# Gated mix of grouped attention and an MLP: two key tiles per stretch of values, eight PSUM banks in rotation, keys split in the second stage

## The chip, the core and the metric

The kernel runs on one core of one Trainium2 chip. A core has a matrix engine (TensorE, PE in the profile, whose weight loads are listed apart as PEld), a vector engine (VectorE, DVE), an activation engine (ScalarE, ACT), GpSimd (POOL) and SyncE (SP), which here only issues transfers. Each engine works through its own list of instructions in order, and waits for the others through semaphores. Matrix products land in PSUM, which has eight banks of 128 x 512 fp32 numbers; PE writes there, DVE and ACT read from there, and everything else is in SBUF or in the chip's memory. The metric is the time of one execution in device microseconds (us).

## What is computed

The input `x` has 2048 tokens of 448 features. Three things are made of it: a gate, attention with 16 query heads that share one key and one value head of 28 features, and an MLP mixer. The output is the gated mix of the last two.

```python
g = sigmoid((x * gate_w).sum(-1, keepdims=True))
# attention: q has 16 heads of 28, k and v have one
scores = einsum("bhqd,bkd->bhqk", q, k) * 28 ** -0.5
a = (softmax(scores) @ v, heads side by side) @ wo
# mixer: a layer norm, 448x448 with gelu, a shift of four channel groups
# by +1, -1, +2, -2 tokens, 448x448, and then
x1 = x + hs
b = x1 + gelu(layernorm(x1) @ w3) @ w4      # 448 -> 1792 -> 448
out = g * a + (1 - g) * b
```

## The kernel before, in words

**Numbers.** Most products are made in fp32r, a one-pass form of fp32 with fewer bits. To keep the accuracy an operand is split into a high part (rounded to fp32r) and a low part (the rest), and three products are added: high x high, high x low, low x high. Names end in `h` and `l` accordingly (`kH`, `kL`, `qh`, `ql`, `w3h`, `w3l`, `onh`, `onl`). The values are multiplied in plain fp32, whose matmul the trace shows as two instructions.

**Order.** The schedule is manual: each engine's instructions run in the order in which the program writes them, and the tile pools add the waits. A tile with `bufs=1` has one buffer, so its next use waits for the last reader of the one before.

**First stage** (to about 130 us). Queries, keys, values and the gate come out of one product per block of 512 tokens; they are written to a scratch tensor `qd` in the chip's memory by `q_out`. Then comes the first half of the mixer (`stage_w1`, `stage_w2`). At its end the keys are fetched: `load_k(b)` (L328) brings block `b` of the keys from `qd` into the tile `kf` with eight DMAs on SP, four copies of the keys at partitions 0, 32, 64 and 96, and `split_k(b)` (L334) makes `kH` and `kL` of it on POOL (L336, L337). The four blocks go through the one `kf`. `kf` is set to 1.0 once, which leaves two rows of ones beside the 28 key features. After them on POOL come the memsets that `split_w_high` (L106) needs for the weights `w3`, and after them on SP the next weight blocks (`load_w34`, L550).

**Second stage, the MLP** (about 130 to 420 us). Four token blocks `b`, 14 feature tiles `f` each: `w3_part` makes a tile of gelu outputs (L130 to L134, L631 to L633), `w4_part` (L641 to L643) adds the tile of two steps before into four accumulators. Between them lie the layer norm of the next block (at f = 9 to 11, through the one-buffer tile `xn`), and work that prepares attention: at b = 1 the tile `khd`, the first `MK` keys set out four times as a block diagonal, and the first queries (`q_load`, `q_split`); from b = 2 on, through `fill`, the maxima of the first unit.

**Attention** (about 420 to 981 us). A unit `u` is a block of 512 tokens and a group of four heads; there are 16. The four heads lie at the partitions 0, 32, 64, 96. For each of the 16 key tiles (128 keys) a step makes:

- scores: for each head one bank, three products of 28 to 30 rows each, on four row tiles of the array at once (L828);
- exponentials: one ACT instruction for each bank, into an SBUF tile `p` (L832);
- values: `pv_group` multiplies the `p` of the key tile two steps before (`LAG`) with `vext`, in which the values stand behind a column of ones; the four heads lie on four column tiles of the array (L808). One bank, `pv`, collects all 16 key tiles of a unit, and DVE then copies it to `o` (L736). Its rows 0, 32, 64, 96 are the sums of the exponentials.

Seven banks rotate among scores and the single products; `pv` has the eighth. The two spare rows of `kH` and `qh` take the row maximum off the scores: `max_part` (L200) takes the maximum over the first `MK` = 64 keys, one product for each of four token tiles (L204, L205), at four different steps of the unit before, and `max_end` writes it to the query tile by DMA. Should a sum be over `LIMIT`, a branch at the end repeats attention with exact maxima.

The sums go to memory and come back as reciprocals on all partitions (`sums_begin`, `recip`: L738, L745, L747, L749); `norm` (L752) multiplies `o` by them on DVE (L754) and splits the result on POOL (L757, L758). At four later steps, `wo_job` (L763) multiplies a token tile with `wo`, again in three products (L769 to L771), and DVE weighs it with the gate and adds it (L778). In the first unit, four last products of the MLP (`w4_job`) stand there. The last unit is normalized by transposes on PE (`tail_sums`, `tail_on`, `tail_back`, `tail_low`).

What decides when a step can start, in a few lines:

```python
bs = [bank(f"s_{4 * k + j}") for j in range(4)]     # next four of the rotation
for i in range(3):
    for j in range(4):
        ... nc.tensor.matmul(bs[j], w, a, start=(i == 0), stop=(i == 2), ...)
if kt in WO_AT: ... wo_job(u - 1, t)
if u + 1 < NU and kt in m_at: ... max_part(u + 1, t, bank)
if k >= LAG:
    pv_group(k - LAG)
```

## Time and profile before

| | us |
|---|---|
| median of 3 runs (lowest, highest) | 994.31 (994.22, 994.57) |
| the profiled execution | 995.8 |
| its span in the profile | 994.0 |
| PE busy | 970.8 |
| ACT busy | 651.9 |
| DVE busy | 287.1 |
| POOL busy | 107.5 |

The profile is taken from one execution. The first page gives the busy time of each engine, the chain of work that ended last (followed backwards from the last instruction), and groups of instructions by line and form. A group's row reads: line, engine, operation, output <- inputs, sizes, count | busy us, mean ns of one | idle time of the engine ahead of it, and what ended it. A row of the timeline reads: start, length, engine, line, operation, with the idle time ahead of it and what ended that in brackets; instructions of one form that overlap are merged (x4). Matmuls are pipelined, so their lengths overlap: the distance from one start to the next is what a matmul takes. A row of busy times by stretch reads: from:to, length, then for PE, PEld, DVE, ACT and POOL the busy us and the instructions, the granted clock of PE, the busy share of the DMA engines, GB/s. A row of waits reads: who <- for whom: us in total, times, longest.

### The profile page before, as it was taken

The numbers are of one execution on the slowest core, as the hardware profiler recorded it, in microseconds if no ns is written. First come the engines' busy times: TensorE is split into PE (matmuls) and PEld (weight loads), VectorE is DVE, ScalarE is ACT, GpSimd is POOL, SyncE is SP. The second block draws the span as 40 slices with busy tenths as digits, with TensorE's granted clock in tenths as the row PEclk, the third lists the DMA queues.
The fourth block names the chain that finished last, engine by engine and source line by source line (L and its number), as shares of the span: only waits on it lengthen the run. The fifth ranks groups of instructions, "written<-read, shape, count | busy, mean of one in ns | idle before, by whom it ended". The sixth has DMA issues, their size and how long they took to land.

```text
span 994.0 us, 18445 instructions
## 1 busy us (share of the span) xinstructions
PE 970.8 (98%) x7251; PEld 562.5 (57%) x7251; DVE 287.1 (29%) x572; ACT 651.9 (66%) x1266; POOL 107.5 (11%) x134
## 2 busy tenths in 40 slices
PE   9999949999999999999999999999999999999997
PEld 6788838888888888843333333333333333333333
DVE  4663424631431431212222222212222221222112
ACT  5542315432232232299999999999998999999895
POOL 2241320100000520040000000000000000000000
PEclk9999969999999999999999999999999999999999
DMA  9703334130210300010000010000010000110001
GB/s 322 244 27 79 114 98 121 44 87 1 40 41 2 77 3 11 1 49 24 13 24 14 19 54 13 24 13 20 27 41 23 14 24 12 42 33 3 12 13 41
DMA packets 38750, 46.19 MB, mean 46 GB/s; under 512 B 8880, under 2 KB 27008, under 8 KB 38656
## 3 DMA queue, kind: packets, MB, share of 16 engines
q1 hardware_dynamic: 35632, 39.47, 13.4%
q10 hardware_dynamic: 3024, 5.47, 1.6%
q8 instruction: 59, 0.97, 0.4%
q14 instruction: 35, 0.29, 0.1%
HBM read 32.85 MB, written 11.67 MB: 45 GB/s over the span
## 4 chain that ended last, share of the span: by engine, by line
PE 94%; DMA 2%; SPq 1%; POOL 1%; DVE 0%; issue 0%; ACT 0%; POOLq 0%; DVEq 0%; ACTq 0%
PE pv L808 25%; PE bank L828 23%; PE acc L642 4%; PE acc L641 4%; PE acc L643 4%; PE g L131 4%; PE g L132 4%; PE g L130 4%; PE bank L769 2%; PE bank L204 2%; SPq L332 1%; PE g L133 1%; PE bank L771 1%; PE g L134 1%; PE bank L770 1%; PE h L130 1%
## 5 line engine op out<-in xcount | busy, mean ns | idle before, releaser
L832 ACT ACTIVATE p<-bank 128x512 f32<-128x512 f32 x1024 | 515.3, 640 | 47.9 <-PE bank L828 45.6
L808 PE MATMUL pv<-p,vext 128*32 128x512 f32 x2048 | 272.9, 604 | 0.0
L828 PEld LDWEIGHTS bank<-qh,kH 30*128 30x128 f32 x1024 | 51.7, 181 | 214.4 <-ACT p L832 212.9
L631 ACT ACTIVATE gh<-g 128x512 fp32r<-128x512 f32 x55 | 32.8, 597 | 183.6 <-PE g L134 183.6
L828 PE MATMUL bank<-qh,kH 30*128 30x512 f32 x1024 | 133.1, 494 | 0.4 <-ACT p L832 0.4
L828 PE MATMUL bank<-qh,kL 28*128 28x512 f32 x1024 | 105.7, 391 | 0.0
L828 PE MATMUL bank<-ql,kH 28*128 28x512 f32 x1024 | 105.6, 388 | 0.0
L633 DVE TENSOR_TENSOR gl<-gf,gh 128x512 fp32r<-128x512 f32 x55 | 38.5, 700 | 165.3 <-ACT gf L632 165.3
L808 PEld LDWEIGHTS pv<-p,vext 128*32 128x32 f32 x2048 | 40.6, 108 | 76.5 <-issue 62.8
L642 PE MATMUL acc<-w4l,gh 128*128 128x448 f32 x220 | 80.4, 366 | 0.0
L641 PE MATMUL acc<-w4h,gh 128*128 128x448 f32 x220 | 80.3, 365 | 0.0
L643 PE MATMUL acc<-w4h,gl 128*128 128x448 f32 x220 | 80.2, 365 | 0.0
L778 DVE SCALAR_TENSOR_TENSOR ot<-bank,gg,ot 128x448 f32<-128x448 f32 x44 | 30.1, 684 | 161.2 <-PE bank L771 122.6
L131 PE MATMUL g<-al,w3h 128*128 128x512 f32 x168 | 66.4, 395 | 0.0
L205 DVE TENSOR_REDUCE mr<-bank 128x4 f32<-128x256 f32 x60 | 25.6, 426 | 141.2 <-PE bank L204 141.2
L130 PE MATMUL g<-ah,w3h 128*128 128x512 f32 x168 | 66.3, 395 | 0.0
L132 PE MATMUL g<-ah,w3l 128*128 128x512 f32 x168 | 66.3, 395 | 0.0
L757 POOL CAST onh<-on 128x512 fp32r<-128x512 f32 x15 | 9.2, 611 | 493.0 <-DVE on L754 458.7
L828 PEld LDWEIGHTS bank<-ql,kH 28*128 28x128 f32 x1024 | 52.6, 185 | 9.1
L828 PEld LDWEIGHTS bank<-qh,kL 28*128 28x128 f32 x1024 | 51.9, 185 | 0.0
L641 PEld LDWEIGHTS acc<-w4h,gh 128*128 128x128 f32 x220 | 41.3, 188 | 4.7
L642 PEld LDWEIGHTS acc<-w4l,gh 128*128 128x128 f32 x220 | 41.3, 188 | 4.1
(196 smaller groups left out, 1096.2 us busy)
## 6 DMA issues: line engine op xcount, KB each, us to landing
qd<-qf ACTq DMA_DIRECT2D x16, 256.0 KB
qr<-qd SPq DMA_DIRECT2D x16, 256.0 KB
rb<-rd SPq DMA_DIRECT2D x15, 256.0 KB
x<-in_x_dram SPq DMA_DIRECT2D x4, 896.0 KB
xd<-xt SPq DMA_DIRECT2D x16, 224.0 KB
w34raw<-in_w_dram SPq DMA_DIRECT2D x7, 512.0 KB
out_dram<-ot SPq DMA_DIRECT2D x15, 224.0 KB
w34raw<-in_w_dram SPq DMA_DIRECT2D x7, 448.0 KB
```

What stands on the lines that cost most here:

```text
L130: nc.tensor.matmul(ps, wh[:, c, :], ah[:, c, :], start=(c == 0), stop=False)
L131: nc.tensor.matmul(ps, wh[:, c, :], al[:, c, :], start=False, stop=False)
L132: nc.tensor.matmul(ps, wl[:, c, :], ah[:, c, :], start=False, stop=False)
L631: nc.scalar.activation(gh, ps, AF.Gelu_apprx_tanh)
L633: nc.vector.tensor_sub(gl, gf, f32(gh))
L641: nc.tensor.matmul(ps, gh[:, tok], w4h[i][:, k, :], start=(f == 0), stop=False)
L642: nc.tensor.matmul(ps, gh[:, tok], w4l[i][:, k, :], start=False, stop=False)
L643: nc.tensor.matmul(ps, gl[:, tok], w4h[i][:, k, :], start=False, stop=(f == stop))
L778: nc.vector.scalar_tensor_tensor(ot_of[n], ps, gg[:, n:n + 1], before, op0=ALU.mult, op1=ALU.add)
L808: nc.tensor.matmul(pv[32 * j:32 * j + 32, :], vext[:, kt, :], ps[j], start=(kt == 0), stop=(kt == NT - 1), tile_position=(0, 32 * j))
L828: nc.tensor.matmul(bs[j], w, a, start=(i == 0), stop=(i == 2), tile_position=(32 * j, 0))
L832: nc.scalar.activation(p, bs[j], AF.Exp, scale=SCALE)
```

## The change

- **Keys split later.** `load_k` and `split_k` leave the end of the first stage. They run in the second token block of the MLP, at f = 0 to 7, each block of keys through a tile of the tag `xn`, which is set to 1.0 each time. `khd` and the first queries move from b = 1 to b = 2, the first unit's maximum from b = 2 on to b = 3.
- **Maxima in one stop.** `MK` goes from 64 to 32, and `max_all` puts the four token tiles into one bank, followed by one DVE reduction; it runs once in a unit, at v = 2.
- **Attention in stretches.** A stretch `v` has two key tiles; a unit has eight. It issues the scores and exponentials of both, then at v = 2 the maximum, at v = 4 to 7 a product with `wo`, and then `values`, the values of the stretch before: both key tiles into one bank. DVE copies the first stretch's sum to `o` in SBUF and adds the others to it. All eight banks rotate; a bank goes to the end of the list when its reader is issued. (`DRAIN` is empty, so `late_exps` issues nothing.)
- **Products with `wo` in fp32.** `norm` no longer splits; `wo_job` multiplies the fp32 `on` with the fp32 `wof`, 32 tokens on each of four column tiles. The splits of `wo` and `on` and `tail_low` are gone. In the tail, DVE adds the last sum to `o` in place of four ACT copies.

```diff
-MK = 64
+MK = 32
-    def max_part(u, t, tile_of): ...
+    def max_all(u, ps):
+        mx_of[u] = late.tile([P, 4, 4], F32, tag="mr", bufs=1, name=f"mr_{u}")
+        for t in range(4):
+            nc.tensor.matmul(ps[:, t * P:(t + 1) * P], qh_of[u][:, t * P:(t + 1) * P], khd, start=True, stop=True)
+        nc.vector.reduce_max(mx_of[u].rearrange("p j t -> p t j"), ps.rearrange("p (t j k) -> p t j k", t=4, j=4), axis=AX.X)
...
-        def load_k(b):
+        def load_k(b, kf):
+            kf_of[b] = kf
+            nc.gpsimd.memset(kf, 1.0)
...
-            split_k(t) if t < 2 else None
-            load_k(t + 1) if t < 2 else None
         stage_w2(NB - 2, third)
-        split_k(2)
-        load_k(3)
-        split_k(3)
...
+                if b == 1 and f in (0, 2, 4, 6):
+                    load_k(f // 2, s2a.tile([P, 512], F32, tag="xn", bufs=1, name=f"kf_{f // 2}"))
+                if b == 1 and f in (1, 3, 5, 7):
+                    split_k(f // 2)
-                if b == 1 and f == 1:
+                if b == 2 and f == 1:
                     nc.gpsimd.memset(f32(khd), 0.0)
...
-        banks = [mm_tile("bank_0"), mm_tile("bank_1"), misc_tile("bank_2")]
+        banks = [mm_tile("bank_0"), mm_tile("bank_1"), misc_tile("bank_2"), max_tile("bank_7")]
...
         def norm(u, o, rb):
-            (on, onh, onl: product on DVE, split on POOL)
+            on_of[u] = s3.tile([P, 512], F32, tag="on", bufs=2, name=f"on_{u}")
+            nc.vector.tensor_mul(on_of[u], o, rb)
...
         def wo_job(u, t, end=None):
-            nc.tensor.matmul(ps, onh[:, tok], woh[:, g, :], start=True, stop=False)
-            nc.tensor.matmul(ps, onh[:, tok], wol[:, g, :], start=False, stop=False)
-            nc.tensor.matmul(ps, onl[:, tok], woh[:, g, :], start=False, stop=True)
+            ps = take()
+            for j in range(4):
+                tok = slice(t * P + 32 * j, t * P + 32 * j + 32)
+                nc.tensor.matmul(ps[32 * j:32 * j + 32, 0:D], on_of[u][:, tok], wof[:, g, :],
+                                 start=True, stop=True, tile_position=(0, 32 * j))
...
+        def values(u, v, add=True):
+            pv = take()
+            for kt in (2 * v, 2 * v + 1):
+                ps = p_of.pop((u, kt))
+                for j in range(4):
+                    nc.tensor.matmul(pv[32 * j:32 * j + 32, :], vext[:, kt, :], ps[j],
+                                     start=(kt % 2 == 0), stop=(kt % 2 == 1), tile_position=(0, 32 * j))
+            if v == 0:
+                o_of[u] = s3.tile([P, 512], F32, tag="o", bufs=2, name=f"o_{u}")
+                nc.vector.tensor_copy(o_of[u], pv)
+            elif add:
+                nc.vector.tensor_add(o_of[u], o_of[u], pv)
+            else:
+                return pv
+            banks.append(pv)
...
+        for k in range(NU * NV):
+            u, v = divmod(k, NV)
+            if v == 6 and u + 2 < NU:
+                q_begin(u + 2)
+                q_fetch(u + 3)
+            for kt in (2 * v, 2 * v + 1):
+                exps(u, kt, scores(u, kt))
+            if v == 2 and sums:
+                norms.append(recip(*sums.pop()))
+            if v == 3 and norms:
+                norm(*norms.pop())
+            if v == M_AT and u + 1 < NU:
+                ps = take()
+                max_all(u + 1, ps)
+                banks.append(ps)
+                max_end(u + 1)
+            job = None
+            if v in WO_AT:
+                if u:
+                    job = wo_job(u - 1, WO_AT.index(v))
+                else:
+                    w4_job(WO_AT.index(v))
+            if job:
+                wo_add(*job)
+            if k:
+                values(*divmod(k - 1, NV))
+                if v == 0:
+                    sums.append(sums_begin(u - 1, o_of[u - 1]))
...
         for t in range(4):
-            nc.scalar.copy(o[:, toks[t]], pv[:, toks[t]])
+            nc.vector.tensor_add(o[:, toks[t]], o[:, toks[t]], pv[:, toks[t]])
```

More of the change, by code (lines that the diff above doesn't have):

```diff
@@ L314, in gated_mix_kernel @@
         nc.gpsimd.memset(vT, 0.0)
-        kf = s1b.tile([P, 512], F32, name="kf")
-        nc.gpsimd.memset(kf, 1.0)
         def rest(g, n, b):
@@ L775, in wo_job, with wo_add @@
             if end:
[L776 removed]
+                end(t, n, ps[:, 0:D], before)
+                banks.append(ps)
                 return
[L778 removed]
+            return n, g, ps, before
+        def wo_add(n, g, ps, before):
+            nc.vector.scalar_tensor_tensor(ot_of[n], ps[:, 0:D], gg[:, n:n + 1], before, op0=ALU.mult, op1=ALU.add)
+            banks.append(ps)
             if g == NG - 1:
                 nc.sync.dma_start(out[0, n * P:(n + 1) * P, :], ot_of[n])
[L782 to L785 removed]
         weigh_x1(NT - 4, NT)
@@ L797, in w4_job @@
             nc.vector.scalar_tensor_tensor(x1[:, n, :], ps, gi[:, n:n + 1], x1[:, n, :], op0=ALU.mult, op1=ALU.add)
-        p_of, pv_of, sums, norms = {}, {}, [], []
-        def pv_group(k):
-            u, kt = divmod(k, NT)
-            if kt == 0:
-                pv_of[u] = max_tile(f"pv_{u}")
-            pv = pv_of[u]
-            ps = p_of.pop(k)
-            for j in range(4):
-                nc.tensor.matmul(pv[32 * j:32 * j + 32, :], vext[:, kt, :], ps[j],
-                                 start=(kt == 0), stop=(kt == NT - 1), tile_position=(0, 32 * j))
-            if kt == NT - 1 and u < NU - 1:
-                sums.append(sums_begin(u, pv_of.pop(u)))
@@ new lines, in gated_mix_kernel, with scores, exps @@
+        p_of, o_of, sums, norms = {}, {}, [], []
+        NV = 8
+        def scores(u, kt):
+            bs = [take() for j in range(4)]
+            for i in range(3):
+                for j in range(4):
+                    for _, _, w, a in score(u, bs[j], j, slice(kt * P, (kt + 1) * P), i=i):
+                        nc.tensor.matmul(bs[j], w, a, start=(i == 0), stop=(i == 2), tile_position=(32 * j, 0))
+            return bs
+        def exps(u, kt, bs):
+            ps = p_of[u, kt] = {}
+            for j in READ:
+                ps[j] = s3.tile([P, 512], F32, tag="p", bufs=PB, name=f"p_{u}_{kt}_{j}")
+                if j in DRAIN:
+                    nc.vector.tensor_copy(ps[j], bs[j])
+                else:
+                    nc.scalar.activation(ps[j], bs[j], AF.Exp, scale=SCALE)
+                banks.append(bs[j])
```

117 lines of the change are left out of this document (32 added, 85 removed).

## Prediction

> **What bounds the kernel now.** I read the page first: the shares of the engines and the chain that ended last.
>
> ```profile
> span 994.0 us, 18445 instructions
> PE 970.8 (98%) x7251; PEld 562.5 (57%) x7251; DVE 287.1 (29%) x572; ACT 651.9 (66%) x1266; POOL 107.5 (11%) x134
> PE 94%; DMA 2%; SPq 1%; POOL 1%; DVE 0%; issue 0%; ACT 0%; POOLq 0%; DVEq 0%; ACTq 0%
> L832 ACT ACTIVATE p<-bank 128x512 f32<-128x512 f32 x1024 | 515.3, 640 | 47.9 <-PE bank L828 45.6
> ```
>
> PE holds the end nearly everywhere, so a saving counts only where PE stops waiting or issues less. The last row, the 1024 exponentials, says that ACT is almost as full inside attention; averages do not settle which binds there. The busy time by stretches does (columns: PE, weight loads, DVE, ACT, POOL, then the granted clock): the end of the first stage, a stretch of the MLP, one unit of attention, and twelve us near the end.
>
> ```profile
> 132.00:144.00 12.00, 0.00 (x0) 0.00 (x0) 0.00 (x0) 0.00 (x0) 3.85 (x5) 0.54 0.24 73
> 144.00:150.00 6.00, 5.75 (x14) 4.50 (x15) 3.56 (x7) 3.46 (x6) 1.45 (x6) 0.50 0.67 224
> 212.00:282.00 70.00, 70.00 (x328) 61.25 (x327) 24.06 (x45) 17.28 (x32) 1.21 (x2) 1.00 0.12 29
> 529.00:564.00 35.00, 35.00 (x340) 13.36 (x341) 7.79 (x18) 32.27 (x65) 1.89 (x2) 1.00 0.06 18
> 949.00:961.00 12.00, 11.76 (x121) 4.42 (x116) 1.03 (x3) 12.00 (x26) 0.74 (x2) 1.00 0.08 25
> ```
>
> There are two places to win: 12 us without any PE work, followed by 6 us at half clock; and attention, where PE is full and ACT has some 3 us of 35 free.
>
> **The key split leaves the first stage.** Waits between 105 and 150 us, then the timeline there:
>
> ```profile
> POOL kH L336 <- DMA kf<-qd: 23.4, 3, 8.0
> PE g L133 <- POOL w3h L106: 13.6, 1, 13.6
> ```
>
> ```profile
> 130.24 0.39 PE L132 MATMUL g<-ah,w3l 128*128 128x512 f32 x1
> ...
> 140.16 0.61 SPq L550 DMA_DIRECT2D w34raw<-in_w_dram  x1
> ...
> 142.57 1.26 POOL L337 TENSOR_TENSOR kL<-kf,kH 128x512 fp32r<-128x512 f32 x1
> 143.89 1.57 POOL L106 MEMSET w3h<- 64x256 f32 x6
> ...
> 144.25 0.79 PE L133 MATMUL g<-ah,w3h 128*128 128x512 f32 x1 [13.62 <-POOL w3h L106]
> 144.70 0.83 ACT L105 CAST w3h<-w34raw 128x768 fp32r<-128x768 f32 x1 [24.11 <-DMA w34raw<-in_w_dram]
> ```
>
> PE stands from 130.24 to 144.25 for a memset (six take 1.57 us) that lies on POOL behind the fourth key split; POOL waited three times, 23.4 us, for key rows, which pass through one buffer in eight small DMAs a block. With the key work gone from there the memset runs as soon as POOL reaches it. The gain is 144.25 - 130.24 - 0.23 (the usual step to the next matmul, shown below) = 13.8 us. The clock fell in the hole: 14 matmuls took 5.75 us; at 0.23 they take 3.2, so 2.5 us more come back. Sum -16.3.
>
> What is late next is the second weight block. Its transfer was issued at 140.16, behind the key DMAs on SP, and its cast began at 144.70, 4.5 us later. Without them SP issues it when its buffer comes free, near 121, and the cast starts near 126; PE needs it only after the 22 products of two tiles (22 x 0.23 = 5.1 us from 128.4). Cost 0, at worst a few us of rest wait (rival 3).
>
> In its new place, the second token block of the MLP, the split issues per key block a memset, eight SP DMAs and two POOL operations. The old chain needed about 10 us a block, so 41 us in all. The row 212 to 282 shows POOL busy for 1.2 of 70 us there, and SP has nothing to issue until that block's f = 11, some 55 us in. The borrowed tile `xn` is wanted by DVE's layernorm at f = 10, 50 us in: 9 us of cover, cost 0; without it, the overrun would delay the next block's activations. `khd`, `qr_0` and the first maximum move a block later, still a block ahead of attention: 0.
>
> **Attention, PE's work.** One plain step, one key tile (what counts are the starts), then a step with a maximum and one with an output product:
>
> ```profile
> 607.29 0.50 PE L828 MATMUL bank<-qh,kH 30*128 30x512 f32 x4
> ...
> 607.64 0.40 PE L828 MATMUL bank<-qh,kL 28*128 28x512 f32 x4
> ...
> 607.87 0.40 PE L828 MATMUL bank<-ql,kH 28*128 28x512 f32 x4
> 608.20 1.07 PE L808 MATMUL pv<-p,vext 128*32 128x512 f32 x8
> ...
> 609.20 0.51 PE L828 MATMUL bank<-qh,kH 30*128 30x512 f32 x4
> ```
>
> ```profile
> 605.99 0.38 PE L204 MATMUL bank<-khd,qh 128*128 128x256 f32 x1
> 606.30 1.06 PE L808 MATMUL pv<-p,vext 128*32 128x512 f32 x8
> ...
> 966.39 0.48 PE L769 MATMUL bank<-woh,onh 128*128 128x448 f32 x1
> ...
> 967.21 1.07 PE L808 MATMUL pv<-p,vext 128*32 128x512 f32 x8
> ```
>
> Scores take .34 + .23 + .33 = .90 and values 1.00, a step 1.90; a maximum adds .31, a product .82. A unit is 16 x 1.90 + 4 x .82 + 4 x .31 = 34.9 us, the 35 of the window: PE's own sum, with no waits in it.
>
> The new stretch has two score groups and then two key tiles of values. Rows where such pairs already stand next to each other:
>
> ```profile
> 420.34 0.40 PE L828 MATMUL bank<-ql,kH 28*128 28x512 f32 x4
> 420.57 0.47 PE L828 MATMUL bank<-qh,kH 30*128 30x512 f32 x3
> ...
> 978.31 1.92 PE L808 MATMUL pv<-p,vext 128*32 128x512 f32 x16
> ```
>
> Group follows group after .23, and a second key tile of values adds 1.92 - 1.06 = .86. Scores of a stretch: .34 + 4 x .23 + .33 = 1.59; values 1.86; in all 3.45 against 3.80 for two steps. The product in fp32 on four column tiles has the form of the values with 448 columns: .86 x 448/512 = .75, and .03 to load: .78 against .82. Below it is .75; above, 3.0 if the four did not run at once. I take .78, since the four of the values do. The four stops for maxima become one, with four products of 128 columns. The nearest rows are the stop of .31 and four loads of 128 columns:
>
> ```profile
> 110.47 0.56 PEld L342 LDWEIGHTS vp<-ident,vT 128*128 128x128 f32 x4
> ```
>
> .56 and .2 for the turns give .75, between .5 and the old 4 x .31 = 1.24. By the Trainium skill (TensorE: Matmul & The Clock Gate, section LDWEIGHTS) a load takes its columns divided by 1.2 in ns; four would take .43, as an estimate, and the sum would be 2 us lower. In the MLP the same merge, for the first unit, gives .75 - 1.24 = -.5 us.
>
> PE's sum for a unit is 8 x 3.45 + 4 x .78 + .75 = 31.5.
>
> **Attention, ACT and the banks.**
>
> ```profile
> 608.36 4.03 ACT L832 ACTIVATE p<-bank 128x512 f32<-128x512 f32 x8 [0.17 <-PE bank L828]
> ...
> 943.32 19.71 ACT L832 ACTIVATE p<-bank 128x512 f32<-128x512 f32 x40 [0.58 <-PE bank L828]
> ```
>
> (19.71 - 4.03)/32 = .49 us per exponential: 3.92 a stretch, 31.4 a unit. On the sums PE and ACT are equal now, so it counts how far one can work ahead of the other. The eight banks serve eight scores, and in between the sum of values, the product and the maximum. How long a sum's bank is held, from the old eviction:
>
> ```profile
> 598.67 0.60 PE L828 MATMUL bank<-qh,kH 30*128 30x512 f32 x4
> ...
> 598.81 0.69 DVE L736 COPY o<-pv 128x512 f32<-128x512 f32 x1 [0.60 <-PE pv L808]
> ...
> 599.65 0.16 PEld L808 LDWEIGHTS pv<-p,vext 128*32 128x32 f32 x8 [0.35 <-DVE o L736]
> ```
>
> It is free .98 us after the next scores begin. In the new rotation it is the last bank of the second score group, wanted at .80: PE waits .18, and its plain stretch is 3.63. Otherwise the seven more DVE evictions a unit cost nothing, DVE being busy 7.8 of 35.
>
> A plain stretch is ACT-bound (3.63 < 3.92). Say the last exponential of a stretch ends at T. Its bank is the third of the next stretch's second group, so PE turns to the values at T + .79, ends them at T + 2.65 and gives ACT the first new scores 1.07 later (607.29 to 608.36) and .05 for the hand-over: T + 3.77. ACT has work until T + 3.92. So the slack is .15 only: a maximum idles ACT for .75 - .15 = .6, the first product for .78 - .15 = .63. From then on PE is behind, 3.63 + .78 = 4.41 or .5 over ACT, three times. Unit: 31.4 + .6 + .63 + 1.5 = 34.1; with a little for each hand-over I take 34.2, -.75 against 34.95 (between the sum of 34.9 and the window of 35.0), 15 times. The last unit has no maximum, and in the old one PE stood for the halves of `on` (L757, L758), which are gone: -1.3. Attention -12.5. POOL's other splits (`wo`, `on`) go at no gain.
>
> Tail: four products of .78 with turns between them, DVE adds in place of ACT copies, the four low halves gone: +.5, between -1 and +1.5.
>
> **Sum.** Made against the profiled execution, 995.8 (span 994.0): -16.3 - 12.5 - .5 + .5 = -28.8. The median of the runs, 994.31, is 1.5 below that execution; 994.3 - 28.8 = 965.5, forecast 966.
>
> **Rivals.**
>
> 1. The norm holds DVE. It is issued in a unit's fourth stretch, ahead of the add that frees the sum's bank.
>
> ```profile
> 601.49 0.24 DVE L745 RECIPROCAL rr<-rt 128x16 f32<-128x16 f32 x1
> ...
> 608.30 0.69 DVE L754 TENSOR_TENSOR on<-o,rb 128x512 f32<-128x512 f32 x1 [0.64 <-DMA rb<-rd]
> ...
> 959.36 0.69 DVE L754 TENSOR_TENSOR on<-o,rb 128x512 f32<-128x512 f32 x1 [8.36 <-DMA rb<-rd]
> ```
>
> From the reciprocal's end to the norm pass 6.57 us, once 8.36. The new reciprocal lies behind the add at the end of the second stretch, 7.8 + .8 + .4 = 9.0 us into the unit; the norm then runs from 15.6 to 16.3, and the add is due near 16.0. These .3 hide where PE waits for ACT's banks anyway (.5). With 8.36 the norm ends 2.1 late and costs about 1.5 a unit: in all 15 units 966 + 22 = 988, in a third of them 974. Place 974 to 988, chance 0.18.
>
> 2. PE and ACT overlap fully, a unit of 31.5 to 33: 19 to 43 us less, 923 to 947. For it: the old loop reached its PE sum exactly, with seven banks. Against: the slack of .15. 0.10.
>
> 3. The change does half of what it says in the first stage: the weight block or POOL keeps half of the hole, 974. 0.05.
>
> 4. Slower: the clock falls in the loop. At half clock a matmul took .41 (5.75/14) in place of .23, so a stretch of 3.45 becomes 6.2, 2.3 above ACT's 3.92. Its place is the wait for a bank, at every stretch; it decides from 28/2.3 = 12 of the 128 stretches on, and a quarter of them gives 966 + 32 x 2.3 = 1040. Against it: the clock of this trace fell in a wait of 13.6 us, and from 949 to 961, with ACT at 12.00 of 12 and PE not full, it stayed at 1.00. The Trainium skill (TensorE: Matmul & The Clock Gate, section A second HAM failure mode: psum-queue depth-cycling) tells of a kernel that cycles through banks, idles briefly between groups and loses clock by it, which the new waits resemble in form. 0.05. That the four tiles of a product run one after another (2.2 x 60 = +132 us) would be slower too: 0.02.
>
> **How the numbers follow.** The main case has 0.60 and its own range 958 to 974 (units of 33.7 to 34.7). The range 948 to 984 adds most of cases 1 and 3 and the near edge of case 2. A measurement of this kernel tells 0.2%, 2 us, from no change. Faster: all but case 4 and a hundredth, 0.92; slower 0.07; same 0.01.
>
> **What would show it.** Right: no idle PE and a clock of 1.00 from 130 to 150 us; L133 not waiting for POOL; the first scores near 403 in place of 420; units near 34.2 with ACT idle for 3, in stretches of 3.6 to 4.1 without a product and 4.4 with one; the product's four matmuls .78 ahead of the values. Wrong: units of 35 and more (then DVE's wait for `rb` is the first suspect), or of 32.

## The result, and the profile after

The changed kernel takes 970.75 us (970.67 to 971.9) beside 994.44 us (994.22 to 996.14) for the kernel before on the same chip: a ratio of 0.9757, with a 95% interval of 0.9745 to 0.9768. The forecast was 966 us with a main case of 958 to 974. The profiled execution took 970.74 us, its span is 968.9. All line numbers from here on are those of the changed kernel: L800 scores, L810 exponentials, L822 values, L826 and L828 DVE's sums of values, L763 the product with `wo`, L753 the norm, L203 the maximum.

The page of the kernel after, span, engines and the exponentials:

```profile
span 968.9 us, 19222 instructions
PE 960.1 (99%) x7571; PEld 589.3 (61%) x7571; DVE 345.7 (36%) x636; ACT 647.0 (67%) x1262; POOL 74.9 (8%) x105
L810 ACT ACTIVATE p<-bank 128x512 f32<-128x512 f32 x1024 | 510.9, 653 | 42.7 <-PE bank L800 42.7
L800 PEld LDWEIGHTS bank<-qh,kH 30*128 30x128 f32 x1024 | 86.2, 182 | 141.8 <-ACT p L810 128.4
```

In the last row the weight loads of the scores wait 128.4 us for ACT. That row alone does not say that PE waits, since in the kernel before it had more:

```profile
L828 PEld LDWEIGHTS bank<-qh,kH 30*128 30x128 f32 x1024 | 51.7, 181 | 214.4 <-ACT p L832 212.9
```

There the weight loads stood while PE still worked on the values, and the starts of the matmuls added up to PE's own 34.9 us a unit. In the kernel after it is the starts that tell of a wait: with the product and the maximum as measured below, the prediction's sum for PE is 8 x 3.45 + 4 x .78 + .59 = 31.3 us, and a unit takes 34.33. The busy time by stretches (columns as in the prediction: from:to, length, PE, PEld, DVE, ACT, POOL, the clock, DMA share, GB/s):

```profile
118.00:144.00 26.00, 26.00 (x123) 22.72 (x122) 15.74 (x31) 11.47 (x20) 0.55 (x2) 1.00 0.47 152
144.00:150.00 6.00, 6.00 (x30) 5.21 (x29) 1.35 (x2) 1.17 (x3) 0.00 (x0) 1.00 0.50 164
212.00:282.00 70.00, 70.00 (x328) 61.16 (x327) 21.89 (x38) 17.27 (x32) 5.69 (x8) 1.00 0.16 39
404.20:407.60 3.40, 3.40 (x23) 1.70 (x23) 0.00 (x0) 3.40 (x9) 2.49 (x2) 1.00 0.85 322
407.60:411.00 3.40, 3.40 (x25) 0.74 (x17) 1.12 (x2) 3.40 (x8) 0.00 (x0) 0.52 0.22 47
```

The hole from 130 to 144 us and the half clock behind it are gone, and the key split now lies in the MLP (POOL 5.69 us of 70 in place of 1.21) with PE still full. There it took 50 us (179.6 to 229.6) where 41 were estimated, and was done 11 us before the layer norm needs `xn`. The last two rows show something that the old loop did not have: the clock at .52 for 3.4 us just after attention begins.

The timeline of the kernel after: the first scores, two starts of a unit, and within a unit a product and the maximum.

```profile
402.13 0.50 PE L800 MATMUL bank<-qh,kH 30*128 30x512 f32 x4
...
408.37 3.28 PE L822 MATMUL bank<-p,vext 128*32 128x512 f32 x16
...
600.86 0.51 PE L800 MATMUL bank<-qh,kH 30*128 30x512 f32 x4
...
602.69 0.96 PE L763 MATMUL bank<-wof,on 128*32 128x448 f32 x8
603.47 1.90 PE L822 MATMUL bank<-p,vext 128*32 128x512 f32 x16
605.30 0.51 PE L800 MATMUL bank<-qh,kH 30*128 30x512 f32 x4
...
609.75 0.50 PE L800 MATMUL bank<-qh,kH 30*128 30x512 f32 x4
...
619.69 0.66 PE L203 MATMUL bank<-khd,qh 128*128 128x128 f32 x4
620.28 1.92 PE L822 MATMUL bank<-p,vext 128*32 128x512 f32 x16
...
644.08 0.50 PE L800 MATMUL bank<-qh,kH 30*128 30x512 f32 x4
```

The first scores start at 402.13 us (419.77 before). A unit takes 644.08 - 609.75 = 34.33 us, a stretch with a product 605.30 - 600.86 = 4.44, the product .78, the stop for the maximum .59. The eight stretches from 609.75 on take 3.69, 4.18, 4.52 (with the maximum), 3.70, 4.94 (the first product), 4.44, 4.42 and 4.45. From the second unit to the fifteenth a unit takes 34.32 to 34.43. The first takes 35.96: in it lies the half clock, at which the first stretch's values took 3.28 us in place of 1.92.

| part, in span time | before | after | difference | predicted |
|---|---|---|---|---|
| up to the first scores | 419.8 | 402.1 | -17.6 | -16.8 |
| first scores to the end of the values | 561.9 | 552.4 | -9.5 | -12.5 |
| end of the values to the end | 12.4 | 14.4 | +2.1 | +.5 |
| span | 994.0 | 968.9 | -25.1 | -28.8 |

(The first line holds the key split and the merged maxima of the MLP. In the other traces of the new loop the first scores start between 401.95 and 402.97 us, so some tenths in this line are scatter.) The profiled execution of before was 1.5 us over its median, so that of the 25.1 some 23.7 are left between the medians.

### The profile page after: what moved, and what is told of

Same layout as the page of the kernel before. It is cut to its first block, busy times and chain, and to the rows that moved or that the text cites. A ratio compares the mean times of both kernels' runs of the same rounds, so it can differ in the third digit from the quotient of the medians.

```text
span 968.9 us, 19222 instructions
## 1 busy us (share of the span) xinstructions
PE 960.1 (99%) x7571; PEld 589.3 (61%) x7571; DVE 345.7 (36%) x636; ACT 647.0 (67%) x1262; POOL 74.9 (8%) x105
## 5 line engine op out<-in xcount | busy, mean ns | idle before, releaser
L810 ACT ACTIVATE p<-bank 128x512 f32<-128x512 f32 x1024 | 510.9, 653 | 42.7 <-PE bank L800 42.7
L822 PE MATMUL bank<-p,vext 128*32 128x512 f32 x2048 | 245.9, 598 | 0.0
L800 PEld LDWEIGHTS bank<-qh,kH 30*128 30x128 f32 x1024 | 86.2, 182 | 141.8 <-ACT p L810 128.4
L800 PE MATMUL bank<-qh,kH 30*128 30x512 f32 x1024 | 168.4, 465 | 0.1
L800 PE MATMUL bank<-qh,kL 28*128 28x512 f32 x1024 | 137.9, 404 | 0.0
L822 PEld LDWEIGHTS bank<-p,vext 128*32 128x32 f32 x2048 | 59.9, 110 | 127.3 <-issue 101.1
L800 PE MATMUL bank<-ql,kH 28*128 28x512 f32 x1024 | 131.3, 389 | 0.0
L828 DVE TENSOR_TENSOR o<-o,bank 128x512 f32<-128x512 f32 x111 | 76.3, 687 | 123.9 <-PE bank L822 72.9
L800 PEld LDWEIGHTS bank<-ql,kH 28*128 28x128 f32 x1024 | 73.6, 185 | 9.6
L800 PEld LDWEIGHTS bank<-qh,kL 28*128 28x128 f32 x1024 | 62.1, 184 | 0.0
L763 PE MATMUL bank<-wof,on 128*32 128x448 f32 x512 | 61.2, 551 | 0.0
```

Of the source, the lines that this page charges most:

```text
L763: nc.tensor.matmul(ps[32 * j:32 * j + 32, 0:D], on_of[u][:, tok], wof[:, g, :], start=True, stop=True, tile_position=(0, 32 * j))
L810: nc.scalar.activation(ps[j], bs[j], AF.Exp, scale=SCALE)
L822: nc.tensor.matmul(pv[32 * j:32 * j + 32, :], vext[:, kt, :], ps[j], start=(kt % 2 == 0), stop=(kt % 2 == 1), tile_position=(0, 32 * j))
L828: nc.vector.tensor_add(o_of[u], o_of[u], pv)
```

## The experiments

Four questions were open: whether the first stage gave what the table's first line says and all of it by the key split; what now limits a unit; whether DVE's wait in the norm (rival 1) is hidden, and by how much; and where the clock's fall and the longer tail come from. Each ratio is to the kernel before on the same chip; "after" is the changed kernel.

### The key split alone

```diff
 kernel BEFORE, with only:
-            split_k(t) if t < 2 else None
-            load_k(t + 1) if t < 2 else None
...
+                if b == 1 and f in (0, 2, 4, 6):
+                    load_k(f // 2, s2a.tile([P, 512], F32, tag="xn", bufs=1, ...))
+                if b == 1 and f in (1, 3, 5, 7):
+                    split_k(f // 2)
```

> The kernel before, with only the key split, khd, the first queries and the first unit's maxima moved one stage or block later; attention as before. Theory (the hole at 130 to 144 us and the half clock after it are the whole price of the split in the first stage, and its new place is free): 994.4 - 17, so 976 to 979, first scores near 402 to 403 us, units of attention 34.96 as before. Rival (the weight block or POOL takes over part of the wait, or the split costs something in the second stage): 982 or more.

Measured: 979.26 us (978.49 to 979.9) beside 995.19, ratio .9843 [.9826, .9859], just above the 976 to 979 expected. The first scores start at 402.32, 17.4 us earlier than in the profiled execution of before (15.9 us between the medians), and the units stay at 34.96. From 118 to 150 us PE is full at a clock of 1.00. So the first line of the table is the key split by itself, within the scatter of the traces, and it is two thirds of the whole gain (15.7 of 24.3 in per mille of the time before).

### Seven banks instead of eight

```diff
-        banks = [mm_tile("bank_0"), mm_tile("bank_1"), misc_tile("bank_2"), max_tile("bank_7")]
+        banks = [mm_tile("bank_0"), mm_tile("bank_1"), misc_tile("bank_2")]
```

> The changed kernel with seven banks in the loop's rotation in place of eight (the eighth comes back for the tail). Theory (the loop is held by banks, not by PE's or ACT's sum: each bank less makes PE wait longer for an exponential): a plain stretch 4.35 us in place of 3.7 to 4.1, one with a product 5.1 in place of 4.44, a unit near 38.6 in place of 34.33, 1035 to 1042 in all. Rival (PE's and ACT's sums of 31.5 hold the loop, the rest is latency that banks do not touch): a unit under 35, at most 980.

Measured: 1049.17 us in a single run, more than the 1035 to 1042 expected, and a unit of 39.18. Instructions and data are the same; one bank less costs 4.85 us a unit. The timeline shows the place:

```profile
600.58 0.51 PE L800 MATMUL bank<-qh,kH 30*128 30x512 f32 x4
...
601.63 4.03 ACT L810 ACTIVATE p<-bank 128x512 f32<-128x512 f32 x8 [1.17 <-PE bank L800]
602.27 0.18 PEld L800 LDWEIGHTS bank<-qh,kH 30*128 30x128 f32 x1 [0.57 <-ACT p L810]
...
605.02 0.50 PE L800 MATMUL bank<-qh,kH 30*128 30x512 f32 x4
```

The second score group lacks one bank, waits .57 for the first exponential, and ACT then idles 1.17 until PE has caught up: each engine waits for the other once in a stretch. With seven banks the limit is the return of the banks, neither PE's sum nor ACT's; what sets the pace with eight is seen in the kernels in which DVE reads one bank in four.

### No products in the loop

```diff
-                if u:
-                    job = wo_job(u - 1, WO_AT.index(v))
+                if u and u < NU - 1:
+                    skipped(u - 1, WO_AT.index(v))
+                elif u:
+                    job = wo_job(u - 1, WO_AT.index(v))
```

This kernel leaves the products with `wo` of units 0 to 13 out of its output (for the first group of heads POOL copies `x1` in their place).

> The changed kernel without the products with wo of units 0 to 13, and without their gated adds (the output lacks those heads). 56 products of .77 us of PE work are gone. Theory (a stretch with a product is PE-bound and one without is ACT-bound at 3.92): units near 32.0, so 2.3 less for each of 14 units, 937 to 941. Rival (PE's sum holds everywhere): units 34.33 - 3.1 = 31.2, 925 to 929.

Measured: 941.75 us in a single run, a unit of 32.11, both just above the expectation. The last three stretches, without their products, take 3.92 to 3.96 us; eight exponentials of .49 are 3.92. The row of the exponentials from 529 to 564 us, idle time behind the second bar:

```profile
L819 ACT ACTIVATE p<-bank 128x512 f32<-128x512 f32 x71 | 35.2, 641 | 0.5 <-PE bank L809 0.5
```

The same row of the kernel after has 3.1 us of idle ACT:

```profile
L810 ACT ACTIVATE p<-bank 128x512 f32<-128x512 f32 x66 | 33.0, 652 | 3.1 <-PE bank L800 3.1
```

Four products cost a unit 34.33 - 32.11 = 2.2, or .55 each of the .78 that PE spends on one; the rest fits into ACT's lead.

### The tail as before

```diff
-            nc.scalar.copy(on_of[u][:, toks[t]], tq[t])
+            nc.scalar.copy(onh[:, toks[t]], tq[t])
...
+            nc.vector.tensor_sub(onl[:, toks[t]], tq[t], f32(onh)[:, toks[t]])
...
-            wo_job(u, t, end)
+            nc.tensor.matmul(ps[:, 0:D], onh[:, tok], woh, start=True, stop=False)
+            nc.tensor.matmul(ps[:, 0:D], onh[:, tok], wol, start=False, stop=False)
+            nc.tensor.matmul(ps[:, 0:D], onl[:, tok], woh, start=False, stop=True)
```

> The changed kernel with the products of the last unit's tail as before (high and low halves, three fp32r products each, the low halves on DVE); the loop keeps fp32 on column tiles. Theory (the tail became 2.1 us longer, 14.45 in place of 12.38 from the end of the values, because four fp32 products of .78 and the turns between them and the transposes stand one behind the other on PE): about 1.5 us less, 969.0 to 969.5, tail 12.7 to 13.2 us. Rival (the DVE adds in place of ACT copies, or the transfers at the end, make it longer): 970.5 to 971.

Measured: 969.97 us (969.25 to 970.46), ratio .9745 [.9729, .9761], above the 969.0 to 969.5 expected. The tail of its trace is 12.68 us against 14.45. In that execution the half clock at the loop's start lasted 6.8 us in place of 3.4 and the first unit 36.91 in place of 35.96, so that the whole shows only a part of the 1.8. The tail's products, first in the kernel after, then here:

```profile
957.32 0.96 PE L763 MATMUL bank<-wof,on 128*32 128x448 f32 x8
958.21 0.33 PE L893 MATMUL bank<-ident,on 128*128 128x128 f32 x1
...
958.47 0.96 PE L763 MATMUL bank<-wof,on 128*32 128x448 f32 x8
...
959.56 1.71 PE L763 MATMUL bank<-wof,on 128*32 128x448 f32 x16
```

```profile
958.64 0.45 PE L921 MATMUL bank<-woh,onh 128*128 128x448 f32 x1
958.93 0.36 PE L922 MATMUL bank<-wol,onh 128*128 128x448 f32 x1
959.13 0.37 PE L923 MATMUL bank<-woh,onl 128*128 128x448 f32 x1
...
959.34 0.27 PE L899 MATMUL bank<-ident,on 128*128 128x128 f32 x1
959.37 0.45 PE L921 MATMUL bank<-woh,onh 128*128 128x448 f32 x1
...
960.08 0.45 PE L921 MATMUL bank<-woh,onh 128*128 128x448 f32 x1
```

A transpose lies between two products in both forms. In fp32r product follows product after .73 and .71; in fp32 after 1.15 and 1.09, although the product itself has .78. From the first product to the end of DVE's last instruction pass 4.77 us in the kernel after and 3.63 here; the other .6 of the 1.8 lie ahead of the products and in the transfer at the end.

### The norm one stretch later

```diff
-            if v == 3 and norms:
+            if v == 4 and norms:
```

> The kernel after with the norm alone one stretch later (v == 4), when the broadcast reciprocals have landed: DVE's 33.6 us of waiting for them goes. Theory (the wait lay beside PE's and ACT's work): unit 34.33 as before, time within 1 us of the kernel after, ratio .975 to .977. The prediction's first rival (the norm holds the add of values, and with it a bank): the unit falls by up to the 2.2 us of the mean wait, the time to 940 to 960 us.

Measured: 970.36 us (969.85 to 971.09), ratio .9747 [.973, .9764]; between the first and the last the units stay at 34.32 to 34.37. The 33.6 us that DVE stood in the norm of the kernel after are gone and nothing is gained: that wait was hidden.

### The first gap filled with warming matmuls

```diff
+            if k == 0:
+                ps = take()
+                for i in range(12):
+                    nc.tensor.matmul(ps[:, 0:256], warm[:, 0:P], warm, start=True, stop=True)
+                banks.append(ps)
```

> The kernel after with twelve small matmuls (the tail's own warming kind, 128x128 weights and 256 columns, into a free bank) behind the scores of the loop's first stretch, where PE otherwise waits for ACT and half the clock follows for 3.4 us. Theory (the fall answers PE's empty time while the loop fills): no fall, the values of stretch 0 take 1.9 us for sixteen instead of 3.28, unit 0 falls from 35.96 to about 34.5, 1.4 us of the whole: about 969.3 us against 970.75. Rival, the fall comes from something else (the DMA that brings the weights of the output product, or the change of stage itself): the clock still falls at that place, unit 0 35.9 or, with the matmuls' own 1.3 us, up to 37.

Measured: 973.53 us (972.04 to 974.36), ratio .9778 [.9761, .9796] beside .9757 [.9745, .9768] for the kernel after: no gain, rather a loss, though the expected thing happened. Its busy time by stretches:

```profile
404.20:407.60 3.40, 3.40 (x37) 2.05 (x29) 0.00 (x0) 3.40 (x8) 3.27 (x3) 1.00 0.92 322
407.60:411.00 3.40, 3.40 (x31) 1.25 (x35) 0.87 (x2) 3.40 (x8) 0.00 (x0) 1.00 0.07 24
```

In the 3.4 us ahead of the place of the fall PE has 37 matmuls in place of 23. No fall of the clock, and a first unit of 34.54. But units 2, 7, 8 and 12 took 34.99, 35.45, 34.6 and 35.69. The timeline of unit 12 shows why:

```profile
834.13 1.11 PE L800 MATMUL bank<-qh,kH 30*128 30x512 f32 x3
834.77 0.69 DVE L753 TENSOR_TENSOR on<-o,rb 128x512 f32<-128x512 f32 x1 [4.25 <-DMA rb<-rd]
835.38 0.68 DVE L828 TENSOR_TENSOR o<-o,bank 128x512 f32<-128x512 f32 x1
836.11 0.49 PE L800 MATMUL bank<-qh,kH 30*128 30x512 f32 x1 [0.87 <-DVE o L828]
```

The broadcast reciprocals landed late; the norm held the sum of values behind it, the sum held its bank, and PE waited .87 for that bank in the middle of a score group. This is exactly the prediction's rival 1, in four units of fifteen. From the reciprocal's start to the norm's the fifteen units of this trace have 6.5 to 8.8 us, and the four longest are the four longer units: 7.7 us go with .3 more, 8.1 with .7, 8.5 with 1.1 and 8.8 with 1.4. In the kernel after they have 6.4 to 7.5, the longest in a unit of 34.43. The same shows once each in two kernels without the warming matmuls: 8.0 us and a unit of 34.88 with the old tail, 8.2 us and a unit of 33.20 in place of 32.11 without products. So after escapes this rival by some tenths of a us, and an execution with slower transfers does not. Why four transfers were late in this trace is open.

### Both together, and with the old tail

> The kernel after with the norm at v == 4 and the twelve warming matmuls together. With the warming matmuls alone the clock did not fall and unit 0 was 34.54, but units 2, 7, 8 and 12 rose to 34.6 to 35.7: there the norm started 7.7 to 8.8 us after the reciprocal (6.4 to 7.5 in the kernel after), because the broadcast reciprocals landed late, and the first product of the unit waited for it. Theory: the two costs are separate, and the norm at v == 4 does not bring the second back as long as the broadcast lands within some 9 us: no fall of the clock, unit 0 34.5, all others 34.33 to 34.4, time 1.4 us under the 970.36 of norm4 alone: 969 us. Rival: the longer units come from the warming matmuls themselves (a bank taken out of turn shifts the rotation of all later ones): single units stay at 35 or more, time 972 or more.

Measured: 969.13 us (969.07 to 969.75), ratio .9735 [.9722, .9748]; first unit 34.52, those between it and the last 34.28 to 34.34, no fall of the clock in the loop. Twice the norm waited for its transfer until 8.2 and 8.5 us after the reciprocal here too, and no unit became longer. The two costs are separate, and a bank taken out of turn costs nothing. The price of the fall, 1.4 us in the traces, stands out less in the times: one of the four executions of the kernel after had a granted clock of .999 over its span, which leaves no room for 3.4 us at half clock, and took 970.67 us all the same.

> The same with the tail's products of the last unit in fp32r from split values, as the kernel before had them. Theory: the tail falls by the 1.8 us that this change alone took from it (14.45 to 12.68), and nothing of the loop moves: 1.8 us under the kernel with norm4 and warming, 967.2 us. Rival: the longer tail of the kernel after was partly the waking of the clock at the loop's end, and nothing is gained: within .5 us of it.

Measured: 968.34 us (967.4 to 968.84), ratio .9722 [.9708, .9735]. The tail fell from 14.54 to 13.01, but only .8 reached the median; in this trace the first scores start .6 later and the first unit has .3 more, and why is open.

### One bank in four read by DVE

All eight banks of a stretch's scores are returned by ACT, one after another. In the next kernels DVE copies the fourth head's scores to SBUF, and ACT makes the exponentials from that copy later (L808 and L815 there).

```diff
-        DRAIN = ()
+        DRAIN = (3,)
...
-            if v == 3 and norms:
+            if v == 4 and norms:
```

> The kernel after with DRAIN = (3,): DVE copies the fourth head's scores of each key tile to SBUF, and ACT exponentiates that copy behind the stretch's other six exponentials, so one bank in four comes free by another engine and earlier; the norm is put one stretch later (v == 4). Theory (what still sets a unit is the order in which ACT gives eight banks back, not ACT's work alone: eight exponentials are 3.9 us a stretch, and a stretch without a product took 4.44): stretches with products fall to about 4.4, a unit from 34.33 to 33.9, 15 times .4 = 6 us, about 964 to 965 us in all. Rival A, ACT's own work and its waits for PE set the loop: unit 34.3 or more, time 969 to 972. Rival B, the sixteen copies a unit of about 1 us each make DVE late with the sums of values: unit 35 or more, above 980.

Measured: 992.72 us (989.09 to 998.0), ratio .9973 [.9948, .9997]: my expectation was wrong by 28 us. The timeline of one unit:

```profile
635.26 1.53 DVE L808 COPY p<-bank 128x512 f32<-128x512 f32 x2 [0.22 <-PE bank L800]
635.44 0.62 PE L800 MATMUL bank<-ql,kH 28*128 28x512 f32 x4
636.71 0.68 DVE L753 TENSOR_TENSOR on<-o,rb 128x512 f32<-128x512 f32 x1
637.53 1.64 PE L763 MATMUL bank<-wof,on 128*32 128x448 f32 x8 [1.48 <-ACT p L810]
```

```profile
PE bank L763 <- DVE on L753: 15.1, 10, 1.8
```

At v == 4 the norm now stands behind two copies that depend on the stretch's own scores, and the product that needs it is PE's next work: PE stands 1.47 to 1.84 us in each of the fifteen units (most took 35.0). The profile puts ten of these waits down to the norm and five, as here, to an exponential; in all fifteen the product starts .15 us after the norm's end. In this trace the clock fell four times more behind such gaps, for 3.4 us each, and three of those units took 36.8 to 37.1 (the fourth is the last unit). The stretches without the gap were shorter, as expected.

The same with the norm left at v == 3:

> The same with the norm left at v == 3. In the kernel after, DVE stands at the norm up to 3.0 us for the broadcast reciprocals, 33.6 us in fifteen units, and nothing that PE or ACT needs at once lies behind it. Here the copies of scores lie behind it. Theory of the hidden wait: the wait now holds a bank and with it the scores, 1.5 to 2 us a unit over the kernel with the norm at v == 4: 25 us more than that (985 to 990 us). Rival, DVE's wait is harmless wherever it is: the same time as with v == 4 (within 2 us).

Measured: 1005.32 us in a single run, 12.6 more than with v == 4, half of the 25 expected. The wait is the expected one, of PE for a bank behind a sum of values that stands behind the norm:

```profile
DVE on L753 <- DMA rb<-rd: 39.4, 15, 4.2
PE bank L800 <- DVE o L828: 25.4, 15, 3.3
```

A wait of DVE that costs nothing in the kernel after lets PE stand for 25.4 us here, because something that PE needs at once was put behind it.

Then with the causes taken out: the reciprocals a stretch earlier, the norm behind the sums of v == 3 and ahead of the copies, the warming matmuls and the old tail.

```diff
-            if v == 2 and sums:
+            if v == 1 and sums:
                 norms.append(recip(*sums.pop()))
-            if v == 3 and norms:
-                norm(*norms.pop())
...
                 values(*divmod(k - 1, NV))
+                if v == 3 and norms:
+                    norm(*norms.pop())
```

> The fourth head's scores through DVE again (DRAIN = (3,)), with what made that slow taken out: the reciprocals one stretch earlier (v == 1), the norm behind the sums of values of v == 3 and so ahead of the copies of the next stretch, the warming matmuls in the first stretch, and the tail in fp32r. In the first try with the norm at v == 4 the norm stood behind two copies, the first product waited 15.1 us for it over the kernel, and the clock fell five times in the gaps; its stretches without that were 3.68, 3.84, 4.55, 3.69, 4.64, 4.42, 4.43 and 4.45, which is 33.70. Theory (the order in which banks come back still costs .6 a unit in the kernel after): unit 33.7, 15 times .63 = 9.5 us under the kernel with norm4, warming and this tail, about 958 us. Rival: DVE, with 16 more copies of .69 us a unit in a fixed order, now holds banks of values or the split of queries: unit 34.3 or more, 967 us or more.

Measured: 964.26 us (963.7 to 964.88), ratio .9684 [.9671, .9698]. Between the first and the last the units are 33.61 to 33.78 (once 34.03), as expected, but the first one is 40.24, with 6.8 us of half clock; in the two kernels before this it had taken 40.32 and 40.38. Its timeline:

```profile
408.37 1.45 DVE L183 CAST qh<-qr 128x512 fp32r<-128x512 f32 x1 [5.08 <-DMA qr<-qd]
409.85 1.00 DVE L184 TENSOR_TENSOR ql<-qr,qh 128x512 fp32r<-128x512 f32 x1
410.78 1.28 DVE L813 COPY p<-bank 128x512 f32<-128x512 f32 x2
...
411.51 0.79 PE L805 MATMUL bank<-qh,kH 30*128 30x512 f32 x2 [5.35 <-DVE p L813]
```

The split of the second unit's queries stands first in DVE's list and waits for a transfer that SP issues behind the 896 KB of `wof`; the copies, and with them PE, wait behind it. In the kernel after the same wait is there, until 407.91 us, but what lies behind it on DVE, the copy of the first sum of values, is not due before 411.79. The last kernel moves that split behind the scores of stretch 1:

```diff
         q_fetch(1)
-        q_begin(1)
-        q_fetch(2)
...
+            if k == 12:
+                (the split of the last wo weights on POOL)
+            if k == 1:
+                q_begin(1)
+                q_fetch(2)
```

> The mended drain kernel with two things moved off the loop's start: the split of the second unit's queries, which stood first in DVE's queue and waited until 408.3 us for its 256 KB to land, so that DVE's copies of scores, and behind them PE, stood from 406.2 to 411.5 us, goes behind the scores of the second stretch; the split of the last output weights on POOL goes to stretch 12. Theory (one wait in DVE's queue, put ahead of the copies, cost the first unit its 40.24 instead of 33.7, and the fall of the clock there followed from PE's empty time): unit 0 34 to 34.5, no fall of the clock, 964.26 less 6 = 958 us (957 to 959.5). Rival: the first unit waits for something else that the drain brings (banks of the first stretch in ACT's order behind the late exponentials): unit 0 above 37, the clock falls again, 961 us or more.

Measured: 958.66 us (958.41 to 959.34) beside 994.21, ratio .9638 [.9625, .9651]. This beats both kernels: 12 us less than the change, and 36 less than before. No fall of the clock in the loop. The first unit is 35.16, not 34 to 34.5; in this trace ACT's table load (1.28 us) stands between the first scores and the first exponential. From 500 to 900 us, first the kernel after, then this one:

```profile
500.00:900.00 400.00, 400.00 (x4148) 177.00 (x4144) 132.14 (x245) 372.12 (x748) 0.00 (x0) 1.00 0.08 25
```

```profile
500.00:900.00 400.00, 395.74 (x4232) 170.65 (x4224) 261.34 (x438) 383.00 (x762) 0.00 (x0) 1.00 0.08 24
```

ACT is busy 383.0 of 400 us in place of 372.1, DVE at twice its work and still a third idle. The exponentials did not become cheaper; those from the copy (the second row) take longer than those from a bank, and back to back they follow after .52 us in place of .48:

```profile
L811 ACT ACTIVATE p<-bank 128x512 f32<-128x512 f32 x768 | 392.9, 644 | 22.9 <-PE bank L801 21.7
L816 ACT ACTIVATE p<-p 128x512 f32<-128x512 f32 x256 | 156.4, 704 | 0.0
```

What is gone are waits for banks. In the second stretch of a unit of the kernel after, the second score group waits twice for ACT:

```profile
614.38 0.18 PEld L800 LDWEIGHTS bank<-qh,kH 30*128 30x128 f32 x1 [0.20 <-ACT p L810]
614.87 0.19 PEld L800 LDWEIGHTS bank<-qh,kH 30*128 30x128 f32 x2 [0.30 <-ACT p L810]
```

In the last kernel that group waits only .17, for DVE's sum of values. The stretch takes 3.84 in place of 4.18 us, the one with the first product 4.58 in place of 4.94, and the other six are the same within .03. That is the whole gain, seven tenths of a us in a unit, for an order in which two engines return the banks. The three stretches behind the first product gain nothing: 4.43 to 4.45 in both kernels, PE's own 3.45 + .78 and a short wait for the bank of the sum.

## Why the prediction was right, and where its sizes were off

**The key split: right.** PE without idle time and a clock of 1.00 from 118 to 150 us, and L133's wait for the memset is gone. The split was put at -16.3 and gave -17.4 by itself in the traces, -15.9 between the medians; with the merged maxima (-.5 predicted) it is -17.6 in the traces, and what the maxima add is too small for these to show. Its new place is free, as argued: PE is full from 212 to 282 us. The rest wait of rival 3 is not there.

**The unit: right in its mechanism, 34.33 for 34.2.** The three limits were named as they were found: ACT's .49 per exponential (32.11 without products), a lead of some tenths that one product uses up, and PE behind ACT from the first product on. The stretches behind the first product were put at 4.41 and are 4.44, the one with the maximum at 3.92 + .6 and is 4.52, the product at .78 and is .78. The first product's stretch and the one ahead of it were put at 4.55 + 3.92 = 8.47 and take 8.64. The wait for the bank of the sum was put at .18 and is .17. What the prediction did not price is the order in which ACT alone returns the banks, in the second stretch and in that of the first product: with a fourth of the banks returned by DVE the unit takes 33.65, although ACT and DVE have more to do. The stop for the maximum was put at .75 from four weight loads of .56 and turns; it took .59. The Trainium skill (TensorE: Matmul & The Clock Gate, section LDWEIGHTS) has a rule by which the four loads would take .43, as an estimate, and with the same .2 for the turns the stop .63; the trace's .59 agrees with that better than with the row that I took.

**The first unit: a term left out, 1.8.** The prediction took .75 off each of fifteen equal units. The first one went from 34.94 to 35.96, since the loop fills: stretch 0 has no values, PE waits for ACT's banks, and the clock then falls for 3.4 us, which is 1.4 of the 1.8. So rival 4's mechanism exists in this kernel, once, in the one place where PE has the least to do; from 500 to 900 us the clock is 1.00 despite a wait at every stretch. The warming matmuls show that PE's thin work there is the cause: all seven traces of the new loop without them have the fall, four of the five with them do not, and the change of stage and the transfer of `wof` are the same in all. The Trainium skill (same page, section A second HAM failure mode: psum-queue depth-cycling) tells of a clock that swings between half and full by short idle times between groups; with after's short waits (from 500 to 900 us the weight loads of the scores wait 151 times for ACT, .8 us at most) the traces do not show that, and with the 1.5 us gaps of the first drain kernel they show four single falls.

**Attention as a whole: -9.5 for -12.5.** 1.8 of the 3.0 are the first unit. The fourteen after it gave .63 each in place of .75, 1.7 in all. The last one gave 1.8 in place of 1.3.

**The tail: a term mis-sized, +2.1 for +.5 (bound +1.5).** The prediction compared a product with a product (.78 against .82) and left the turns as they were. The trace shows 1.15 and 1.09 from product to product, against .73 and .71 in fp32r, with a transpose between them in both. With the old form the tail fell by 1.8 (and by 1.5 in a second pair of kernels).

**Rival 1: right as a mechanism, and closer than its price tells.** In the kernel after the norm waits 33.6 us in all and next to none of it shows; moving it away gains nothing. Where the norm starts 7.7 us and more after the reciprocal's start, it decides, up to 1.4 us a unit, as the warming kernel has it in four units. The prediction put the point between the 6.57 and 8.36 us of the old trace (counted from the reciprocal's end, .25 later), and its price of 1.5 for a late one is near the 1.1 and 1.4 of the two latest.

**Rival 2: excluded** by the units of 34.33, and the reason given (the small lead) fits the run without products, where ACT idles .5 of 35 us in place of 3.1.

The sum of the differences, 1.8 + 1.7 - .5 in attention, 1.6 in the tail and -.8 ahead of it, is 3.8 beside the 3.7 between the spans (-28.8 and -25.1). The forecast missed 4.8 because it took the sum off the median, while it was made in an execution 1.5 us longer; the execution of after stands at its own median. In which part of the old trace those 1.5 us lie is open. Some of it may be half clock: later executions of before with a granted clock of .989, which the profiled one has too, average 996.0 us, those with .991 or .992 average 995.1.

## What to carry to other kernels

When two engines share a rotation of buffers and their sums are nearly equal, ask in which order the buffers come back and who returns them: here a unit took 39.2, 34.3 or 33.65 us with seven banks, with eight, and with eight of which a second engine returned a fourth. A wait in an in-order list costs nothing or tens of us, depending on what stands behind it; before an instruction is put on an engine with free time, list the waits ahead of it and what waits for it, at the loop's start too. And look at the first round of a loop separately: it has other gaps than the rest, and the clock may answer them.

## What the runs showed of the hardware

In the loop the clock fell in stretches of 3.4 us or 6.8 us. In all kernels with the new loop that fell at its start, the fall began between 406.5 and 409.0 us, and twelve small matmuls in the first stretch were enough to keep it at 1.00 in the traces of four kernels, but not in the one where PE stood 5.35 us behind them. In the first drain kernel a single gap of 1.47 to 1.84 us per unit was followed by a fall in four units and not in the other eleven; what decides between them stays open.

The broadcast of the reciprocals (256 KB to 128 partitions, through the chip's memory) took 6.5 to 8.8 us from the reciprocal's start to the norm's within one execution of the warming kernel, and 6.4 to 7.5 us in that of the kernel after; why is open. A schedule with room for the usual length has none for the longest.
